# Fewer plain w_out units between the gating stages, more seven-product end groups, and w_sp blocks converted by ScalarE column by column

## The chip, the cores and the metric

The kernel runs on one core of a Trainium2 chip. The metric is device time in microseconds for one execution, lower is better. A core has five engines with a queue each: TensorE (PE; its weight loads are listed as PEld), VectorE (DVE), ScalarE (ACT), GpSimd (POOL) and SyncE (SP, which here only issues DMAs). An engine takes its own queue strictly in the order in which it was written, so an instruction that waits holds up all that stand behind it on that engine.

## The reference

The function is a pre-norm block with two parts. Part A is a linear attention with a memory over four segments of 512 tokens; part B is a gated MLP, and the change lies in part B (and in the scales that it uses).

```python
h  = x + A(layernorm(x))
z  = gelu(layernorm(h) @ w_in)              # 2048 tokens x 3584
z1 = z[..., :1792]
z2 = layernorm(z[..., 1792:])
g  = einsum('ts,bsf->btf', w_sp, z2) + b_sp[None, :, None]   # mixes the 2048 tokens
out = h + (z1 * g) @ w_out                  # w_out: 1792 x 1024
```

All inputs and the output are bfloat16.

## The kernel before, in words

The program is recorded as a list per engine. `_Recorder.record` works out for each instruction which earlier ones on other engines, and which DMAs, it must wait for, from the memory that it reads and writes; `emit` (lines 196 to 241) then writes the waits and the instructions. Every instruction therefore carries line 210 in the profile, and groups are told apart by the names of their tiles. Nothing reorders the work: the order in the source is the order on each engine.

The stages from the middle on are these.

**z2 and z1 stages.** The z2 stage computes the second half of z and its layernorm; the list `aux` (function `at`) hangs other work on its groups, among it the squares of w_sp for a scale (`sp_norm`, `scale_of`, `scale_end`) and the z1 weight blocks' sums (`sz_sum`, GpSimd). The z1 stage (`z1_step`, line 1198) computes z1 transposed into `Z1T` (feature blocks 0 to 13 of 128 rows, 2048 tokens), with `todo1` (function `on`) as its list of extra work.

**Gating stage, pair 0 and pair 1** (`gate`, line 1086). The 2048 output tokens are taken in two pairs of 1024. A pair is a product of a 2x2 block matrix of w_sp (b11, b12, b21, b22: 512 tokens each, as float16 in `BH`) with z2 (float16, `Z2H`), computed with seven block products instead of eight. The sums of w_sp blocks are t1 = b12 - b11, t2 = b22 - t1, t3 = b22 - b12, t4 = b21 - t2 (`SUMS`, line 1060); those of z2 are SS[0] to SS[3], made for each feature group g of 0 to 6 by `s_sum` (called ss1 to ss4). A product is 8 matmuls of 512 columns into one of the eight PSUM banks. The first product P1 (`p1`, with b11) is copied out, scaled, by ScalarE (`copy1` into the tile tmp_s) because several outputs need it alone; after that the b21 product (`p2`) is accumulated into the same bank. GpSimd adds the bias rows `BROW` to the copy (tmp_s1b), VectorE combines banks with these (`stt`: scalar_tensor_tensor into tmp_u) and multiplies by z1 (`out`; `c11` is the pair of these two for the first quadrant). Pair 0 writes bfloat16 back into Z1T, pair 1 float16 into `Z1X`, which is the same memory.

**Units** (lines 1267 and 1331 to 1361) stand between the two gating stages. A unit is 128 tokens by 512 output columns: 14 matmuls of the gated z1 with w_out (`out_unit`), VectorE's add of the residual tile `FIN`, and a store. The residual was loaded by `fin_load` from the output buffer. There are four FIN tiles, so a load waits for the store of four units back. Loads, stores, and the loads of w_out's second half (`WO1`) all go through ScalarE's DMA queue. Behind the units' adds stand the conversions of pair 1's w_sp blocks: DMA transposes on SP (`sp_load`, four for each block, of 128 of its 512 rows each) bring them as bfloat16 into the memory of pair 0's blocks as these come free; `sp_half` scales and casts a whole block on VectorE (4096 elements in a row), `sp_sum` makes the sums. ScalarE computes squares of w_out (`wo_norm`) and of b_sp (`brow_sq`) for scales (`scale_y`, `scale_w`). All of pair 0, 1024 tokens by 1024 columns, is computed by 16 units.

**End groups** (lines 1363 to 1501). Pair 1's product with w_out is again computed by seven block products, in four groups of 2 x 128 tokens, 49 matmuls each. The blocks of w_out are scaled to float16 by ScalarE (`ob_scale`) and their sums made by VectorE (`ob_sum`) inside gating stage 1, by `each1`; the sums of the gated z1 (`y_sum`, tiles SY) belong to each group. ScalarE copies the first product out (`o_p1`), GpSimd adds the residual to it three times (`o_adds`, tiles OT4).

Of the kernel before, what the change touches and what calls it, by code (L numbers as in the profile page):

```python
# [12 lines left out]
T = 2048  # L13
# [20 lines left out]
class _Recorder:  # L34


    def __init__(self, nc):
# [9 lines left out]
        self.out_dmas = []  # L47
        for k in ENGS:
            setattr(self, k, _Eng(self, k))
# [37 lines left out]
    def record(self, eng, name, args, kw, dma=None):  # L87
# [94 lines left out]
        if dma is not None:  # L182
# [4 lines left out]
            key = (aps_out[0] is sb, sb.tensor.name, int(sb.offset))  # L187
# [8 lines left out]
    def emit(self):  # L196
# [9 lines left out]
        def run(eng, e):  # L206
            for op in self.ops[eng]:
                for o in op.waits:
                    e.wait_ge(o.dma if o.dma is not None else sems[o.eng], o.val)
                ins = getattr(e, op.name)(*op.args, **op.kw)  # L210
                if op.dma is not None:
                    ins.then_inc(op.dma, 16)
                elif op.sig:
                    ins.then_inc(sems[eng], 1)
# [44 lines left out]
def bass_sequential_preLN__memory_aug_infini_attn__mixer_gmlp__prompt_kernel(  # L259
# [126 lines left out]
    SQ = b3("sq", [128, 16], F32)  # L386
# [6 lines left out]
    TW, YS, INVY, SCW, INVO = [b3(k, [128, 1], F32) for k in ("tw", "ys", "invy", "scw", "invo")]  # L393
    SQY = tens("sqy", [128, 28], F32, 768)
    BSQ = tens("bsq", [128, 2], F32, 896)
# [5 lines left out]
    WO1 = [tens("w_out1%d" % i, [128, 7, 512], BF16, o * K) for i, o in enumerate((30, 4))]  # L401
    WO0H = [tens("w_out0h%d" % i, [128, 7, 512], F16, o * K) for i, o in enumerate((54, 198))]
    FIN2 = tens("fin2", [128, 4, 2, 2, 512], BF16, 14 * K)
    OT4 = [[tens("ot%d%d" % (i, k), [128, 512], F32, (o + 2 * k) * K) for k in range(4)] for i, o in enumerate((38, 118))]
# [533 lines left out]

    def scale_of(k, n, b):
# [4 lines left out]
        if k:  # L944
            dve.reciprocal(TOP[:], TOT[:])
        else:
            pool.tensor_tensor(TOP[:], TOT[:], MHZ[:], ALU.pow)
# [53 lines left out]
    at(37, pool.tensor_copy, SQB[:, 0:16], SQ[:])  # L1001
# [6 lines left out]
    at(20, pool.tensor_copy, SQB[:, 0:14], SQZ[:])  # L1008
    at(25, scale_of, 1, 14, None)
    at(25, scale_end, 1)  # L1010
    for k in range(8):
# [3 lines left out]
    for k in (1, 2, 3, 4):  # L1015
        at(35 + k, sz_sum, 0, k)
# [4 lines left out]
    for it in todo:  # L1021
# [6 lines left out]
        if it == (0, 12):  # L1028
            sp_norm_load(0)
# [29 lines left out]

    SUMS = {"t1": ("b12", "b11"), "t2": ("b22", "t1"), "t3": ("b22", "b12"), "t4": ("b21", "t2")}  # L1060
# [25 lines left out]
    def gate(pr, seam=lambda: None, mid=lambda: None, each=lambda g, k: None):  # L1086
        inv, zo = (INV[0], Z1T) if pr == 0 else (INVY, Z1X)
# [31 lines left out]
        if not pr:  # L1119
            p1(2)  # L1120
        seam()
        p2(0)
        c11(0)
        for g in range(7):
# [6 lines left out]
            ss(4, g)  # L1131
# [3 lines left out]
            if 1 - pr <= g <= 3:  # L1135
# [14 lines left out]
            out(u3, g, 1, t2)  # L1150
            if not g:
                ss(1, 1)
                ss(2, 1)
            if g < 6:
# [23 lines left out]
    def out_unit(u, wsl, q=sp):  # L1178
        tc, lo, w = u
        b = next_bank()  # L1180
        mm8(PS[:, b, 0:w], lambda i: Z1T[:, i, tc * 128:(tc + 1) * 128], wsl, n=14)
        fin = fins[u]
        dve.tensor_tensor(fin[:, 0:w], fin[:, 0:w], PS[:, b, 0:w], ALU.add)
# [7 lines left out]
    wout = B_w_out.rearrange("(c p) n -> p c n", p=128)  # L1191
# [55 lines left out]
    on(1, 7, scale_of, 0, 16, None)  # L1247
    on(2, 2, scale_end, 0)
    for k, g, r in (("b11", 6, 3), ("b12", 6, 3), ("b22", 8, 3), ("b21", 12, 3)):
# [17 lines left out]
    units = [(tc, 0, 512) for tc in range(6)] + [(tc, 512, 512) for tc in range(8)] + [(tc, 0, 512) for tc in (6, 7)]  # L1267
# [9 lines left out]
    def z1_norm(g, k):  # L1277
        for h in range(k and 2):
            r, o = 2 * g + (k > 2), 1024 + 512 * h
            if k != 2:  # L1280
                act.activation(bank(7), Z1T[:, r, o:o + 512], ACTF.Square, accum_out=SQY[:, 2 * r + h:2 * r + h + 1])

    gate(0, seam, mid, z1_norm)
    pool.tensor_copy(TW[:], TOT[:])
    fin_load(units[0], act)
    fin_load(units[1], act)
    for k in ("b11", "b12", "b22", "b21"):
        for j in range(4):
            sp_load(1, k, j)
    brow_load(1, act)  # L1290
    for i in range(2):
        act.dma_start(WO1[i][:], wout[:, 7 * i:7 * i + 7, 512:D])
# [240 lines left out]
```

## Time and profile before

| | us |
|---|---|
| Median of three runs | 758.01 (757.65 to 758.52) |
| The profiled execution's own time | 757.02 |
| Its span, first to last instruction | 755.3 |
| Gating stage, pair 0, on the weight loads | 489.1 to 574.0 |
| Units | 574.0 to 622.4 |
| Gating stage, pair 1 | 622.4 to 709.3 |
| End groups | 709.3 to 752.4 |

The granted TensorE clock was 1.000 over the span. The profile is of one execution; "busy" for TensorE is modelled, since matmuls overlap, so rates are better read from the starts of successive weight loads. A wait is read as "who waited <- who released it". The stage limits in the table are where the weight loads change from one pair of tiles to the next.

### The profile page before, as it was taken

Reading aid. Unit: us, or ns where it says so; the run is one execution under the profiler, and the core shown is the slowest. Engines: PE = TensorE matmul, PEld = TensorE weight load, DVE = VectorE, ACT = ScalarE, POOL = GpSimd, SP = SyncE. Lnnn points to the kernel's source line nnn. Section 1 sums busy time; section 2 is a strip of 40 time slices with the busy share of each in tenths; the row PEclk is TensorE's granted clock in tenths of the full one; section 3 lists DMA queues with packets and bytes.
Section 4 is the critical chain, followed back from the end, with each engine's and each line's share of the span. In section 5 each row is a group of like instructions: output and inputs, shape, how many; then the busy total and the mean of one; then the engine's idle time right before and its main releaser. Section 6 shows DMA issues by size and latency. Waiting matters only on the chain.

```text
span 755.3 us, 13486 instructions
## 1 busy us (share of the span) xinstructions
PE 748.4 (99%) x5470; PEld 357.9 (47%) x5470; DVE 573.4 (76%) x1013; ACT 421.4 (56%) x519; POOL 294.0 (39%) x450
## 2 busy tenths in 40 slices
PE   8999999999999999999999999999999999999998
PEld 4445455555554445555554444444444444443444
DVE  5585589768974576768896796998895575999876
ACT  6777877787777767226994879723330525300000
POOL 2564456555654333010049988522120001122342
PEclk9999999999999999999999999999999999999999
DMA  9654556454424331678640026320029950001111
GB/s 304 173 160 91 85 78 139 94 79 92 113 58 96 115 72 43 178 195 254 195 141 0 1 56 126 68 86 1 0 41 171 234 196 15 0 1 55 64 49 56
DMA packets 136783, 75.09 MB, mean 99 GB/s; under 512 B 98064, under 2 KB 126480, under 8 KB 136720
## 3 DMA queue, kind: packets, MB, share of 16 engines
q1 hardware_dynamic: 129184, 67.14, 36.9%
q10 hardware_dynamic: 7536, 7.08, 3.2%
q8 instruction: 43, 0.70, 0.4%
q14 instruction: 20, 0.16, 0.1%
HBM read 42.74 MB, written 8.39 MB: 68 GB/s over the span
## 4 chain that ended last, share of the span: by engine, by line
PE 88%; DVE 10%; DMA 1%; issue 1%; POOL 0%; ACT 0%; ACTq 0%; DVEq 0%; POOLq 0%
PE ps L210 88%; DVE z1x L210 3%; DVE tmp_u L210 3%; DVE ss L210 2%; DMA wv<-in_A_wv_dram 1%; DVE tmp_s1b L210 1%; DVE z2h L210 0%; POOL ot L210 0%; DVE sy L210 0%; POOL sy L210 0%; ACT L210 0%; DVE ot L210 0%; DVE fin L210 0%; ACTq L210 0%; DVEq L220 0%
## 5 line engine op out<-in xcount | busy, mean ns | idle before, releaser
L210 ACT ACTIVATE e<-ps 128x2048 bf16<-128x2048 f32 (+1 forms) x96 | 152.7, 1590 | 41.7 <-PE ps L210 41.5
L210 POOL TENSOR_SCALAR_AFFINE_SELECT e<-e 128x512 bf16<-128x512 bf16 x128 | 90.6, 721 | 131.4 <-ACT e L210 131.4
L210 PE MATMUL ps<-win,hnT 128*128 128x448 bf16 x512 | 98.4, 353 | 0.0
L210 POOL TENSOR_TENSOR tmp_s1b<-tmp_s,brow 128x512 f32<-128x512 f32 x28 | 33.6, 1203 | 129.7 <-DVE tmp_u L210 57.4
L210 PEld LDWEIGHTS ps<-win,hnT 128*128 128x128 bf16 x512 | 49.6, 98 | 46.3 <-issue 0.2
L210 PE MATMUL ps<-xnT,wk 128*128 128x512 bf16 x256 | 60.8, 381 | 0.0
L210 PE MATMUL ps<-xnT,wq 128*128 128x512 bf16 x256 | 60.5, 379 | 0.0
L210 PE MATMUL ps<-wv,xnT 128*128 128x512 bf16 x256 | 59.8, 380 | 0.4 <-DVE xnT L210 0.3
L210 DVE TENSOR_TENSOR zt<-ps,zt 128x512 f32<-128x512 f32 x70 | 48.2, 689 | 15.7 <-PE ps L210 12.1
L210 PE MATMUL ps<-wo,oT 128*128 128x512 bf16 x256 | 58.0, 380 | 0.0
L210 ACT ACTIVATE z<-ps 128x448 bf16<-128x448 f32 x60 | 30.6, 548 | 35.0 <-PE ps L210 35.0
L210 PE MATMUL ps<-w_out,z1T 128*128 128x512 bf16 x224 | 48.6, 379 | 0.0
L210 DVE BATCH_NORM_STATS2 zst<-z 128x6 f32<-128x448 bf16 x64 | 38.0, 612 | 10.9 <-ACT z L210 10.9
L210 PEld LDWEIGHTS ps<-v,e 128*128 128x128 bf16 x1280 | 38.8, 96 | 14.0 <-issue 6.5
L210 DVE RECIPROCAL rd<-ps 128x16 f32<-128x16 f32 x32 | 8.0, 250 | 47.1 <-PE ps L210 46.9
L210 ACT ACTIVATE tmp_s<-ps,invy 128x512 f32<-128x512 f32 x7 | 4.8, 687 | 68.0 <-POOL tmp_s1b L210 37.8
L210 PE MATMUL ps<-v,e 128*128 128x33 bf16 x1280 | 42.2, 178 | 0.0
L210 POOL TENSOR_TENSOR sz<-wzh 128x512 f16<-128x512 f16 x28 | 34.5, 1231 | 8.4 <-PE ps L210 8.4
L210 PEld LDWEIGHTS ps<-wo,oT 128*128 128x128 bf16 x256 | 24.0, 98 | 27.6
L210 PEld LDWEIGHTS ps<-xnT,wk 128*128 128x128 bf16 x256 | 22.6, 98 | 29.9 <-issue 5.0
L210 ACT ACTIVATE z1T<-zt,inv 128x512 bf16<-128x512 f32 x42 | 29.0, 715 | 13.1 <-DVE zt L210 13.1
L210 PEld LDWEIGHTS ps<-wv,xnT 128*128 128x128 bf16 x256 | 23.1, 98 | 27.3 <-DVE xnT L210 0.8
(206 smaller groups left out, 1478.0 us busy)
## 6 DMA issues: line engine op xcount, KB each, us to landing
sj<-in_B_w_sp_dram SPq DMA_DIRECT2D x16, 512.0 KB, 3.6
xch<-in_A_x_dram SPq DMA_DIRECT2D x16, 256.0 KB, 3.4
xr<-in_A_x_dram SPq DMA_DIRECT2D x16, 256.0 KB, 3.9
out_dram<-hch SPq DMA_DIRECT2D x16, 256.0 KB, 2.6
win<-in_B_w_in_dram SPq DMA_DIRECT2D x4, 896.0 KB, 5.3
wz<-in_B_w_in_dram SPq DMA_DIRECT2D x6, 512.0 KB, 7.9
wo<-in_A_wo_dram SPq DMA_DIRECT2D x1, 2048.0 KB, 8.4
fin<-out_dram ACTq DMA_DIRECT2D x16, 128.0 KB, 3.0
```

The costliest lines, as they stand in the source:

```text
L210: ins = getattr(e, op.name)(*op.args, **op.kw)
```

## The change

Pair 0 is no longer finished by units alone. Eight units do tokens 0 to 255 and 512 to 767 (token blocks 0, 1, 4, 5 of 128, by two column halves); the other half of pair 0 goes to two more end groups, so six end groups in place of four. Pair 0's gating therefore writes float16 with the final scale, as pair 1's does, and the scale that it needs (YS) is computed in the z1 stage. The squares of w_out move into gating stage 0 (`w_norm`), half of them of a tile `WOT` that is loaded piece by piece for it on ScalarE's queue. In the units, pair 1's w_sp blocks b11, b12 and b22 are cast by ScalarE (b11 by rows, the other two by 128-column pieces as each transpose brings them) and the sums t1, t2, t3 are made by column pieces, t3 and ss after the last unit; t4 is made inside gating stage 1. The transposes come in the order b11, b21, b12, b22. In gating stage 1 the third P1 product is issued early, and c11 and ss4 of group 0 late. w_out's b12 and b22 blocks are loaded with runs of 256 bytes into the token columns that the units have finished with; t4 of w_out is made in the first end group. WO1 lies elsewhere, and its loads stand ahead of those of BROW. Waits on the same DMA semaphore are merged, and some DMAs share one (`group`).

```diff
             for op in self.ops[eng]:
+                need = {}
                 for o in op.waits:
+                    if o.dma is not None:
+                        need[o.dma] = max(need.get(o.dma, 0), o.val)
+                for o in op.waits:
+                    if o.dma is not None and o.val < need[o.dma]:
+                        continue
                     e.wait_ge(o.dma if o.dma is not None else sems[o.eng], o.val)
                 ins = getattr(e, op.name)(*op.args, **op.kw)
                 if op.dma is not None:
...
-    WO1 = [tens("w_out1%d" % i, [128, 7, 512], BF16, o * K) for i, o in enumerate((30, 4))]
+    WO1 = [tens("w_out1%d" % i, [128, 7, 512], BF16, o * K) for i, o in enumerate((38, 30))]
...
-    FIN2 = tens("fin2", [128, 4, 2, 2, 512], BF16, 14 * K)
-    OT4 = [[tens("ot%d%d" % (i, k), [128, 512], F32, (o + 2 * k) * K) for k in range(4)] for i, o in enumerate((38, 118))]
+    FIN2 = tens("fin2", [128, 6, 2, 2, 512], BF16, 14 * K)
+    OT4 = [[tens("ot%d%d" % (i, k), [128, 512], F32, (o + 2 * k) * K) for k in range(4)] for i, o in enumerate((46, 118))]
...
         if k:
-            dve.reciprocal(TOP[:], TOT[:])
-        else:
-            pool.tensor_tensor(TOP[:], TOT[:], MHZ[:], ALU.pow)
+            pool.tensor_single_scalar(TZ[:], TOT[:], float(2 * T * FH * D * D), ALU.mult)
+        pool.tensor_tensor(TOP[:], TOT[:], MHZ[:], ALU.pow)
...
+    def sp_cast(k, j):
+        c = slice(128 * j, 128 * j + 128)
+        act.activation(BH[k][:, :, c], RAW[k][:, :, c], ACTF.Copy, scale=SC[0][:])
+
+    def sp_csum(o, j):
+        a, b = SUMS[o]
+        c = slice(128 * j, 128 * j + 128)
+        dve.tensor_tensor(BH[o][:, :, c], BH[a][:, :, c], BH[b][:, :, c], ALU.subtract)
...
-        inv, zo = (INV[0], Z1T) if pr == 0 else (INVY, Z1X)
+        inv, zo = INVY, Z1X
...
-        if not pr:
-            p1(2)
+        p1(2)
         seam()
         p2(0)
-        c11(0)
+        if not pr:
+            c11(0)
...
-            ss(4, g)
+            if g or not pr:
+                ss(4, g)
...
-            if 1 - pr <= g <= 3:
+            if 1 <= g <= 3:
...
-            out(u3, g, 1, t2)
+            if pr and not g:
+                ss(4, 0)
             if not g:
                 ss(1, 1)
                 ss(2, 1)
+            out(u3, g, 1, t2)
+            if pr and not g:
+                c11(0)
             if g < 6:
...
-        mm8(PS[:, b, 0:w], lambda i: Z1T[:, i, tc * 128:(tc + 1) * 128], wsl, n=14)
+        mm8(PS[:, b, 0:w], lambda i: Z1X[:, i, tc * 128:(tc + 1) * 128], wsl, n=14)
         fin = fins[u]
-        dve.tensor_tensor(fin[:, 0:w], fin[:, 0:w], PS[:, b, 0:w], ALU.add)
+        dve.scalar_tensor_tensor(fin[:, 0:w], PS[:, b, 0:w], IY[:], fin[:, 0:w], ALU.mult, ALU.add)
         q.dma_start(out2d[tc * 128:(tc + 1) * 128, lo:lo + w], fin[:, 0:w])
...
+    on(9, 3, pool.tensor_tensor, TOT[:], TOT[:], TZ[:], ALU.mult)
+    on(9, 3, pool.tensor_tensor, TOP[:], TOT[:], MHZ[:], ALU.pow)
+
+    def y_scale():
+        dve.tensor_single_scalar(TOP[:].bitcast(I32), TOP[:].bitcast(I32), 0x7F800000, ALU.bitwise_and)
+        dve.tensor_single_scalar(YS[:], TOP[:], 8192.0, ALU.mult)
+        dve.tensor_tensor(INVY[:], INV[0][:], YS[:], ALU.mult)
+        dve.reciprocal(IY[:], YS[:])
+
+    def brow_scale():
+        for k in range(2):
+            act.activation(BROW[k][:], BROW[k][:], ACTF.Copy, scale=YS[:])
+
+    on(11, 2, y_scale)
+    on(11, 3, brow_scale)
     for k, g, r in (("b11", 6, 3), ("b12", 6, 3), ("b22", 8, 3), ("b21", 12, 3)):
...
-    units = [(tc, 0, 512) for tc in range(6)] + [(tc, 512, 512) for tc in range(8)] + [(tc, 0, 512) for tc in (6, 7)]
+    units = [(tc, lo, 512) for lo in (0, 512) for tc in (0, 4, 1, 5)]
...
+    def w_sq(c, v):
+        act.activation(bank(7), v, ACTF.Square, accum_out=SQY[:, c:c + 1])
+
+    def w_norm(g, k):
+        h = 4 * g + k
+        if h % 2:
+            w_sq(14 + h // 2, WOT[:])
+        else:
+            act.dma_start(WOT[:], wout[:, h // 2, 512:D])
+            for c in ([h // 2 - 2] if h >= 4 else []) + ([h // 2] if h >= 24 else []):
+                w_sq(c, WO0[c // 7][:, c % 7, :])
+
+    def w_scale(n):
+        if n == 0:
+            pool.tensor_copy(SQB[:], SQY[:])
+        if n == 1:
+            b = 3
+            pe.matmul(PS[:, b, 0:28], ONES[:], SQB[:], start=True, stop=True)
+            dve.tensor_reduce(out=TOT[:], in_=PS[:, b, 0:28], axis=mybir.AxisListType.X, op=ALU.add)
+            dve.tensor_single_scalar(TOT[:], TOT[:], 1e-30, ALU.max)
+            pool.tensor_tensor(TOP[:], TOT[:], MHZ[:], ALU.pow)
+        if n == 3:
+            dve.tensor_single_scalar(TOP[:].bitcast(I32), TOP[:].bitcast(I32), 0x7F800000, ALU.bitwise_and)
+            dve.tensor_single_scalar(SCW[:], TOP[:], 8192.0, ALU.mult)
+            dve.tensor_tensor(INVO[:], YS[:], SCW[:], ALU.mult)
+            dve.reciprocal(INVO[:], INVO[:])
...
+    gate(0, seam, mid, w_norm)
+    for u in units[:2]:
+        fin_load(u, act)
+    for i in range(2):
+        act.dma_start(WO1[i][:], wout[:, 7 * i:7 * i + 7, 512:D])
+    brow_load(1, act)
+    for k in ("b11", "b21", "b12", "b22"):
         for j in range(4):
             sp_load(1, k, j)
-    brow_load(1, act)
...
+    for r in range(4):
+        sp_part("b11", r)
+
+    rot["n"] = 0
     for n, u in enumerate(units):
-        if n + 2 < 16:
+        if n + 2 < 8:
             fin_load(units[n + 2], act)
         out_unit(u, (lambda i: WO0[i // 7][:, i % 7, :]) if u[1] == 0 else
                  (lambda i: WO1[i // 7][:, i % 7, :]), act)
...
+        w_scale(n)
...
-        if n == 1:
-            sp_half("b11")
-        if n == 4:
-            sp_half("b12")
-            sp_sum("t1")
-        if n == 6:
-            sp_half("b22")
-            sp_sum("t3")
-        if n == 8:
-            sp_sum("t2")
-        if n == 10:
+        if n == 2:
             sp_half("b21")
-            sp_sum("t4")
-        if n == 12:
-            scale_w()
-        if n == 13:
-            for k in range(1, 4):
-                s_sum(k, 0)
...
+        if n in (4, 5):
+            for j in (2 * n - 8, 2 * n - 7):
+                sp_cast("b12", j)
+                sp_csum("t1", j)
+        if n == 5:
+            brow_scale()
+        if n in (6, 7):
+            for j in (2 * n - 12, 2 * n - 11):
+                sp_cast("b22", j)
+                sp_csum("t2", j)
+    for k in range(1, 4):
+        s_sum(k, 0)
+    for j in range(4):
+        sp_csum("t3", j)
+
+    W4 = {"b12": (Z1T, 0), "b22": (Z1T, 1), "t1": (Z2, 0), "t2": (Z2, 1), "t3": (Z1T, 0), "t4": (Z2, 2)}
...
+    def ob_load(k):
+        i = 7 if k == "b22" else 0
+        R.group = (k,)
+        w = wout[:, i:i + 7, 512:D].rearrange("p c (a b t) -> p c a b t", a=2, b=2)
+        o = ob(k, 0, 7, False).rearrange("p (c a) b t -> p c a b t", a=2)
+        for a in range(2):
+            for b in range(2):
+                sp.dma_start(o[:, :, a, b], w[:, :, a, b])
+        R.group = None
...
+    GR = [(0, 2), (0, 3)] + [(1, j) for j in range(4)]
...
+    for n, o in enumerate(("t1", "t2", "t3")):
+        for m in range(4):
+            jobs.setdefault(((2, 2, 2, 3, 3, 3, 3, 4, 4, 4, 5, 6)[4 * n + m], 0), []).append((ob_sum, o, 2 * m))
...
+    ob_load("b12")
+    ob_load("b22")
+    gate(1, mid=mid, each=each1)
...
-    fin_in(2)
-    fin_in(3)
+    for g in range(2, 6):
+        fin_in(g)
     o_p1(0)
-    for x in range(1, 4):
-        y_sum(x, 0, 6, 7)
     o_adds(0)
-    o_prod(3, o_s(2, 0), "t2", True, cs=range(6))
+    o_p1(1)
+    o_prod(3, o_s(2, 0), "t2", True)
     o_p2(0)
     o_c11(0)
...
-    for g in range(4):
+    for g in range(6):
         bb, bc = 3 + g % 2, 5 + g % 2
-        last = ((bc, 0, 512),) if g < 3 else ((bc, 0, 384), (7, 384, 512))
+        last = ((bc, 0, 512),) if g < 5 else ((bc, 0, 256), (7, 256, 512))
...
+        if g == 0:
+            for m in range(4):
+                ob_sum("t4", 2 * m)
+        if g < 3:
+            o_p1(g + 2)
         o_prod(bb, o_s(3, g), "t3", False)
-        if g < 3:
-            o_p1(g + 1)
-        elif g == 3:
-            o_p2(3)
+        if g < 4:
+            o_adds(g + 1)
+            o_p2(g + 1)
```

## The prediction

> **What bounds the kernel now.** I read the page first (busy shares, then the chain that ended last), then the weight loads of TensorE in the last gating stage, then the timeline between the two gating stages.
>
> ```profile
> PE 748.4 (99%) x5470; PEld 357.9 (47%) x5470; DVE 573.4 (76%) x1013; ACT 421.4 (56%) x519; POOL 294.0 (39%) x450
> PE 88%; DVE 10%; DMA 1%; issue 1%; POOL 0%; ACT 0%; ACTq 0%; DVEq 0%; POOLq 0%
> ```
>
> TensorE carries 88% of the chain, VectorE 10%. That 10% is one stretch, 634.9 to 716.1 us: the second gating stage. The waits of its weight loads (window 622 to 709; us in total, times, longest):
>
> ```profile
> PEld ps L210 <- DVE tmp_u L210: 4.3, 6, 1.1
> ```
>
> So TensorE idles there for VectorE's tmp_u, the sums out of the product banks. And the timeline between the stages (start, us, engine, what; in brackets the idle time before it):
>
> ```profile
> 573.97 24.05 PEld L210 LDWEIGHTS ps<-w_out,z1T 128*128 128x128 bf16 x112
> 574.89 10.38 SPq L210 DMA_TRANSPOSE b22r<-in_B_w_sp_dram  x4
> 577.61 1.11 ACTq L210 DMA_DIRECT2D w_out<-in_B_w_out_dram  x2
> 578.75 4.14 ACTq L210 DMA_DIRECT2D fin<-out_dram  x1
> 585.31 9.83 SPq L210 DMA_TRANSPOSE b21r<-in_B_w_sp_dram  x4
> 590.90 0.69 DVE L210 TENSOR_TENSOR fin<-fin,ps 128x512 bf16<-128x512 bf16 x1 [7.40 <-DMA fin<-out_dram]
> 591.38 0.33 ACTq L210 DMA_DIRECT2D fin<-out_dram  x1
> 594.56 0.69 DVE L210 TENSOR_TENSOR fin<-fin,ps 128x512 bf16<-128x512 bf16 x1 [2.07 <-DMA fin<-out_dram]
> ...
> 622.36 3.34 PEld L210 LDWEIGHTS ps<-b11h,z2h 128*128 128x128 f16 x16
> 624.50 0.69 ACT L210 ACTIVATE tmp_s<-ps,invy 128x512 f32<-128x512 f32 x1 [14.33 <-PE ps L210]
> 625.82 1.61 PEld L210 LDWEIGHTS ps<-b21h,z2h 128*128 128x128 f16 x8
> 627.54 1.61 PEld L210 LDWEIGHTS ps<-t2h,ss 128*128 128x128 f16 x8
> ```
>
> To be seen: 16 units run from 573.97 to 622.36, 48.4 us, without a gap. Eight matmuls of 512 columns take 627.54 - 625.82 = 1.72 us (1.727 over longer stretches): 0.2158 us each. The third fin load was issued at 578.75 behind the two w_out loads and VectorE got it only at 590.90; the next fin load needs the first store landed and arrives at 594.56. All this is hidden now, since the w_sp conversions have 48 us and run on VectorE. The copy at 624.50 follows the first product at once, and the b21 product (which adds onto the bank that was copied) need not wait.
>
> **What the Trainium skill says.** "DMA: Bandwidth & Descriptors", section "Queues, rings and completion order": SP and ACT own one ring each per DMA engine, consumed in ring order, and an engine takes turns between rings by packets. The trace agrees: the fin load waited out 1.8 MB ahead of it on ACT's ring (12.1 us from issue to use; the page's median to landing is 3.0). "TensorE: Matmul & The Clock Gate", section "Step-by-step: what each phase is for": about 216 ns from one 512-column matmul to the next; here 215.8. "ScalarE: Activation LUTs", section "What ACT_TABLE_LOAD costs": neighbouring ACTIVATEs overlap by about 93 ns; here casts of 128x1024 last 1.14 us and follow each other after 1.05. "DMA: Bandwidth & Descriptors", section "Specifications": full rate needs runs of 512 B; the new b12/b22 loads of w_out have runs of 256 B. No run here shows them; the nearest row is wz with 256 B runs, 256 KB in 4.8 us. Taking some 2 us of that as fixed, 2.8 us for 1024 runs give an estimated 20 us for the 7168 runs, issued from about 597 and wanted from 618: covered, with little to spare.
>
> **The change, part by part.**
>
> *Products.* Units fall from 16 x 14 = 224 to 112 matmuls; end groups rise from 4 x 49 = 196 to 294. Net -14 x 0.2158 = **-3.0 us**. This is certain.
>
> *Norms moved.* Gate 0 keeps 28 ScalarE squares (0.79 us with the read) and gains 14 loads of 128 KB on ACT's queue. ScalarE idles 8.5 us per group there, so it is free except at the end: after the last copy (561.26) three load-then-square rounds of about 4.5 us follow, so the last square ends near 575.2 instead of 567.1. Then come the fin loads (574.4 before, now 575.2). The w_out loads stand ahead of brow now: about 576.5 against 577.6. The scale chain moved into the z1 stage is four VectorE operations (0.65 us) and two ScalarE ones (1.3 us), where VectorE has gaps of only 0.17 us: 0 to 0.5, I take **+0.2**. Reading z1 as f16 and scaling in the final add (0.75 against 0.69 us) cost nothing on TensorE.
>
> *Units.* The SP queue issues b21 at 571 (its last reader), then b12, b22: 12 transposes, 25.9 us from 569.2 to 595.1 before, so until about 597, landed by 602. Not the bound. ScalarE is. Its queue now holds, in order: fin loads, w_out, brow, four b11 casts (4.3 us), then per unit a fin load, the output store (which waits for VectorE's add) and two casts. VectorE in turn queues two column sums behind each add, and they wait for those casts. From unit 4 on it is a loop: store issue 0.45, casts 1.05 + 1.14, sum 0.05 + 0.65, next add 0.75: **4.1 us a unit**, TensorE 3.02.
>
> When does it start? Fin load 2 follows w_out and brow in ACT's ring: I take 590.0 (590.9 before; w_out is issued about 1 us sooner). Fin load 4 waits for store 0, is issued at 590.5, lands 3.1 later, unit 4's add ends at 594.3. Stores 5, 6 and 7 are issued by 598.85, 602.95, 607.05; the last casts end at 609.25; only then comes the gating copy, 0.69: 609.9. The b21 product accumulates into that copied bank, so it waits. TensorE, unhindered, would get there at 573.97 + 24.2 + 3 x 1.727 = 603.35. **+6.55 us.** (w_out's second half, wanted at 587.6 and landing near 589.5, stalls unit 4 by 1.8; that is inside these 6.55.) Sums and the two ss blocks end at 611.25, the b21 product at 611.6: hidden behind it.
>
> *Gate 1.* VectorE works 10.3 us a group (656.04 to 667.89 less three sums of 0.51), TensorE 12.1, or 10.4 in groups 0 and 4 to 6, where the P1 product came earlier. After the wait VectorE still owes ss3, four t3 sums, four t4 sums (0.61 each, 5.5 us) and the postponed c11 and ss4. Walked through by these durations, the group-1 t3 product waits 1.9 us net for the add before it (VectorE 17.4 us after the start, TensorE 15.5). Group 2 and 3 sums fit; the three at group 4 exceed it by 1.8. Together 3.7 against 2.4 before (the six waits sum to 4.3, of which the weight-load pipeline regains 0.2 to 0.4 each: 622.36 to 709.34 is 86.98, less 392 x 0.2158): **+1.3**.
>
> *End.* 0.8 us is lost at 713.8 and 716.1 now, because the first adds run uncovered. A second P1 product ahead covers them, and the first group is ready earlier: **-0.7**. The four t4 sums (2.5 us) end 1.3 us before their product. The last bank's half is 256 columns instead of 128: **+0.1**.
>
> Sum: -3.0 + 0.2 + 6.55 + 1.3 - 0.7 + 0.1 = +4.4. On the profiled execution's 757.02 (span 755.3) that is 761.4; the median 758.01 lies 1.0 above it: **762.4**.
>
> **Rivals.** 0.2% (1.5 us) is about what a measurement of this kernel can tell from no change.
>
> *A, ScalarE's loop delays the b21 product,* as above, 760 to 765: chance 0.50. For it: the 7.40 us wait at 590.90. Against it: the transposes' order differs, so the ring may drain sooner.
>
> *B, the loop keeps pace: faster.* One mechanism: fin load 2 lands early, so casts follow the loads and the copy ends before 603.35. The copy follows fin load 2 by 19.9 us, so the point is a landing at 583.4. Then -3.0 + 0.2 + 1.3 - 0.7 + 0.1 = -2.1: 755.9. For it: 1 MB of transposes used to be issued from 574.9, while now b21 has been issued by 576.7. Against it: the w_out loads alone bring 1.8 MB, and the 576 to 590 stretch moved 64 to 364 GB/s. Chance 0.20.
>
> *C, half of the wait:* landing near 586.5, about 758: chance 0.14.
>
> *D, VectorE or a load is later still:* the brow issue blocks ACT as the fin load did at 578.75 (4.14 us), so the b11 casts start 4 us later and all behind them; or the 256 B loads hold up the scaling in group 1 and the copy behind it. 765 to 769: chance 0.16.
>
> **How the numbers follow.** Faster 0.20 (B), within 0.2% 0.12 (most of C), slower 0.68 (A, D, the rest of C). The range from 755.2 to 766.5 takes in B, C, A and part of D. A alone: 760 to 765.
>
> **What would show it.** Right: the b21 product of gate 1 idle before it, released by ScalarE's tmp_s, some 5 to 8 us; fin adds in the units waiting for DMA fin; stores of units 5 to 7 some 4 us apart; about 3.7 us of VectorE waits in gate 1. Wrong: fin load 2 landing before 584; the b21 product following at once; the t2 product waiting for the t2 sums because b22 lands late; end groups longer than 10.6 us each.

## The result, and the profile after

The changed kernel takes 767.45 us (median of four runs, 765.96 to 768.62) against 758.07 of the kernel before on the same chip (757.65 to 758.52): ratio 1.0123, 95% interval 1.0104 to 1.0141. It is 9.4 us slower. The forecast was 762.4 us, 755.2 to 766.5: the right side, by about half of what came, and the median lies 1 us outside the range.

The profiled execution took 768.62 us, its span is 766.9. Section 1 of the page (busy time) and section 4 (chain that ended last) now read:

```profile
PE 750.1 (98%) x5455; PEld 358.6 (47%) x5455; DVE 585.1 (76%) x1032; ACT 421.7 (55%) x517; POOL 301.1 (39%) x450
PE 85%; DVE 9%; DMA 2%; issue 1%; ACT 1%; ACTq 1%
```

DMA, ScalarE (ACT) and its queue (ACTq) hold more of the chain than before: 2%, 1% and 1% against 1%, 0% and 0%. The busy time of TensorE did not fall although it has 15 matmuls fewer: some ran at half rate, as shown below (2.5 us), and the part ahead of gating stage 0, which is left out below, has 1.9 us more of it (488.7 against 486.7). The waits of the weight loads from the units to the end (window 574 to 766; total, times, longest) say who is in the chain:

```profile
PEld ps L217 <- ACT tmp_s L217: 6.5, 1, 6.5
PEld ps L217 <- DVE tmp_u L217: 5.3, 5, 2.1
PEld ps L217 <- issue: 3.6, 13, 0.3
PEld ps L217 <- DMA w_out<-in_B_w_out_dram: 2.4, 2, 2.1
PEld ps L217 <- DVE ot L217: 1.1, 1, 1.1
```

One wait of 6.5 us is for ScalarE's tmp_s, the copy of the first gating product. It is the wait that the prediction named. The 13 "issue" gaps of 0.28 us are new, and are the half rate. The timeline of ScalarE between the stages (start, us, engine, what; in brackets the idle time before it) shows how the copy comes so late:

```profile
585.34 0.45 ACTq L217 DMA_DIRECT2D out_dram<-fin  x1
...
593.82 0.34 ACTq L217 DMA_DIRECT2D fin<-out_dram  x1
...
597.97 0.34 ACTq L217 DMA_DIRECT2D fin<-out_dram  x1
598.35 0.70 ACTq L217 DMA_DIRECT2D out_dram<-fin  x1
599.10 1.15 ACT L217 ACTIVATE b12h<-b12r,sc 128x1024 f16<-128x1024 bf16 x1 [11.76 <-issue]
...
602.70 0.35 ACTq L217 DMA_DIRECT2D out_dram<-fin  x1
...
606.70 0.37 ACTq L217 DMA_DIRECT2D out_dram<-fin  x1
...
610.73 0.34 ACTq L217 DMA_DIRECT2D out_dram<-fin  x1
...
613.20 0.67 ACT L217 ACTIVATE tmp_s<-ps,invy 128x512 f32<-128x512 f32 x1
```

For 11.8 us before its first b12 cast at 599.10 ScalarE computes nothing: its queue stands at fin loads that need a landed store (593.82, 597.97) and at stores that need an add. The adds of units 2 and 4 on VectorE waited for these loads:

```profile
593.34 0.75 DVE L217 SCALAR_TENSOR_TENSOR fin<-ps,iy,fin 128x512 bf16<-128x512 f32 x1 [9.39 <-DMA fin<-out_dram]
597.16 0.75 DVE L217 SCALAR_TENSOR_TENSOR fin<-ps,iy,fin 128x512 bf16<-128x512 f32 x1 [0.58 <-DMA fin<-out_dram]
```

Then the stores come 4.0 us apart, and the copy is at the end of that row. What TensorE does with it, in the weight loads from the end of the units on:

```profile
602.38 5.06 PEld L217 LDWEIGHTS ps<-b11h,z2h 128*128 128x128 f16 x24
613.92 0.13 PEld L217 LDWEIGHTS ps<-b21h,z2h 128*128 128x128 f16 x2 [6.48 <-ACT tmp_s L217]
614.32 0.15 PEld L217 LDWEIGHTS ps<-b21h,z2h 128*128 128x128 f16 x1 [0.28 <-issue]
...
619.86 1.61 PEld L217 LDWEIGHTS ps<-t1h,ss 128*128 128x128 f16 x8
...
635.70 1.41 PEld L217 LDWEIGHTS ps<-t3h,ss 128*128 128x128 f16 x8 [2.15 <-DVE tmp_u L217]
```

After the wait, the 16 matmuls of the b21 and t2 products take 619.86 - 613.92 = 5.94 us, or 2.49 more than 16 x 0.2158 = 3.45. Twelve steps in a row, 614.32 to 619.43, are 0.43 us each, twice the usual, and the granted clock from 613.92 to 619.43 is 0.50. The Trainium skill describes this in "TensorE: Matmul & The Clock Gate", "Part 1: The HAM clock gate": after an idle window of some 3.4 us the clock falls to half, and it comes back after about 3.4 us of work, which varies from run to run. The trace agrees in kind: 6.5 us idle, then half rate until 619.43, 5.5 us.

Where the time went. The profiled execution's gate 0 starts at 491.55 against 489.13, all of it from the first 20 us, where TensorE's granted clock was 0.91 against 1.00 and 1.37 us against 0.68 were spent on a load of wv. Code there is the same, and in the experiments below, which share that code, gate 0 starts between 489.0 and 490.4; so I leave it out and count from the start of the units (573.97 before, 576.39 after) to the end of the span: 181.33 us before, 190.51 after, **+9.18**, close to the 9.4 of the medians.

| from the units' start on, us | predicted | measured |
|---|---|---|
| 14 matmuls fewer | -3.0 | -3.02 |
| b21 product later than unhindered (29.38 after the start) | +6.55 | 37.53 - 29.38 = +8.15 |
| 16 matmuls at half rate | not seen | +2.49 |
| gate 1 waits for VectorE | +1.3 | 3.84 net against 2.4: +1.44 |
| start of the end stage | -0.7 | 0.74 lost against 0.54: +0.2 |
| tail | +0.1 | -0.1 |
| sum | +4.25 | +9.16 |

### The profile page after: what moved, and what is told of

Its sections match the earlier page's. It is cut to its first block, busy times and chain, and to the rows that moved or that the text cites. A ratio compares the mean times of both kernels' runs of the same rounds, so it can differ in the third digit from the quotient of the medians.

```text
span 766.9 us, 13491 instructions
## 1 busy us (share of the span) xinstructions
PE 750.1 (98%) x5455; PEld 358.6 (47%) x5455; DVE 585.1 (76%) x1032; ACT 421.7 (55%) x517; POOL 301.1 (39%) x450
## 4 chain that ended last, share of the span: by engine, by line
PE 85%; DVE 9%; DMA 2%; issue 1%; ACT 1%; ACTq 1%
PE ps L217 85%; DVE tmp_u L217 3%; DVE z1x L217 2%; DMA out_dram<-fin 2%; DVE ss L217 1%; ACTq L217 1%; DVE z2h L217 1%; DMA wv<-in_A_wv_dram 1%; DVE tmp_s1b L217 1%; ACT b12h L217 1%; ACT b22h L217 0%; DVE fin L217 0%; DVE ot L217 0%; DVE sy L217 0%; ACT b11h L217 0%
## 5 line engine op out<-in xcount | busy, mean ns | idle before, releaser
L217 ACT ACTIVATE tmp_s<-ps,invy 128x512 f32<-128x512 f32 x14 | 9.6, 685 | 97.2 <-POOL tmp_s1b L217 70.8
L217 POOL TENSOR_TENSOR ot<-ot,fin 128x512 f32<-128x512 f32 x18 | 22.9, 1301 | 42.7 <-ACT ot L217 22.2
L217 ACT ACTIVATE ot<-ps,invo 128x512 f32<-128x512 f32 x6 | 4.1, 687 | 61.8 <-PE ps L217 61.8
L217 DVE TENSOR_TENSOR z1x<-tmp_u,z1T 128x512 f16<-128x512 f32 x42 | 36.5, 868 | 1.4
```

## The experiments

Two theories were to be told apart. *Mine*: the order of ScalarE's queue makes the loss, because stores, loads and casts in one queue wait for each other. *The rivals*: the half rate of TensorE is the larger part; or VectorE, which has the same row of sums, would have been as late without ScalarE. Medians of before on the chip used were 758.3 to 758.6 us throughout.

**TensorE kept busy.** 24 extra matmuls into an unused bank fill most of the wait; their results are not used.

```diff
         p1(2)
+        if pr:
+            for x in range(24):
+                pe.matmul(bank(7), a_blk(0, 0, 0)[:, x % 8, :], BH["b11"][:, x % 8, :], start=True, stop=True)
         seam()
```

> The changed kernel with 24 extra matmuls of 512 columns into a bank that nobody reads, placed between the third P1 product and the b21 product of gating stage 1, so that TensorE works through most of the 6.4 us in which it now waits for ScalarE's copy. Nothing else moves: the copy is as late as before. Theory (the 16 weight loads after the wait run at half rate because TensorE had stood still): they run at 0.216 us each again, 2.5 us are saved, 764.9 against 767.4. Rival (the slow stretch comes from something else near it, such as the GpSimd and VectorE work at that place): no gain, 767.4.

Measured: 766.66 us (766.3 to 766.99), ratio 1.011 [1.0093, 1.0127]. The weight loads that waited, from the end of the units on:

```profile
612.84 1.41 PEld L217 LDWEIGHTS ps<-b21h,z2h 128*128 128x128 f16 x8 [1.19 <-ACT tmp_s L217]
615.16 1.41 PEld L217 LDWEIGHTS ps<-t2h,ss 128*128 128x128 f16 x8 [0.91 <-DVE ss L217]
619.78 1.41 PEld L217 LDWEIGHTS ps<-t3h,ss 128*128 128x128 f16 x8 [1.49 <-DVE tmp_u L217]
634.02 1.41 PEld L217 LDWEIGHTS ps<-t3h,ss 128*128 128x128 f16 x8 [2.47 <-DVE tmp_u L217]
```

The half rate is gone, but little of its 2.5 us came back: 0.8 us by the medians, where the runs of the changed kernel themselves lie 2.7 us apart, and 0.1 us from the units' start to the end of the two profiled executions (190.43 against 190.51, with the copy itself 0.5 us later in the first). The t2 and t3 products, which followed at once after the slow stretch, now wait 0.91 and 1.49 us for VectorE, and group 1 waits 0.3 longer. So the slow stretch mostly lay over a lateness of VectorE that was there anyway.

**VectorE converts b12 and b22 whole**, as in the kernel before. This undoes the part of the change that gave the column casts to ScalarE.

```diff
-        if n in (4, 5):
-            for j in (2 * n - 8, 2 * n - 7):
-                sp_cast("b12", j)
-                sp_csum("t1", j)
+        if n == 4:
+            sp_half("b12")
+            sp_sum("t1")
...
-        if n in (6, 7):
-            for j in (2 * n - 12, 2 * n - 11):
-                sp_cast("b22", j)
-                sp_csum("t2", j)
+        if n == 7:
+            sp_half("b22")
+            sp_sum("t2")
```

> The changed kernel with one part undone: b12 and b22 are scaled and cast by VectorE as whole blocks (1.28 us each) and t1, t2 made as whole blocks (2.3 us each), b12 after unit 4, b22 after unit 7; ScalarE has no casts in the units but those of b11. Theory (the copy is late because ScalarE's stores and casts alternate with VectorE's adds): the copy follows the store of unit 7 at about 604.4, the b21 product does not wait, TensorE keeps its clock: about 8.5 us less, 759. Rival (b22's transposes land late and bound the t2 sums whoever casts them): the wait moves to the t2 product and 764 or more remain.

Measured: 761.29 us (760.58 to 763.04), 1.0044 [1.0029, 1.0059]: 6.2 of the 9.4 us are back. The weight loads at the t2 and t1 products:

```profile
609.20 0.13 PEld L217 LDWEIGHTS ps<-t2h,ss 128*128 128x128 f16 x2 [2.98 <-DVE ss L217]
...
612.57 1.39 PEld L217 LDWEIGHTS ps<-t1h,ss 128*128 128x128 f16 x7 [0.25 <-issue]
```

The b21 product follows at once. The t2 product does wait 2.98 us for VectorE's sums, and half rate follows that too, until 612.57. ScalarE's queue, in which stores and casts alternate, is the larger cause; without it VectorE is still late by 3 us.

**Eight FIN tiles**, so that no load waits for a store; all eight loads stand ahead of the units, four of them ahead of w_out.

```diff
-        k = len(fins) % 4
+        k = len(fins) % 8
-    for u in units[:2]:
+    for u in units[:4]:
         fin_load(u, act)
     for i in range(2):
         act.dma_start(WO1[i][:], wout[:, 7 * i:7 * i + 7, 512:D])
     brow_load(1, act)
+    for u in units[4:]:
+        fin_load(u, act)
-        if n + 2 < 8:
-            fin_load(units[n + 2], act)
```

> The changed kernel with eight residual tiles in place of four: units 0 to 3 load theirs ahead of w_out, units 4 to 7 behind the bias rows, none waits for a store. Stores and casts stay on ScalarE. Theory (the loop of store, casts, sums and add starts late because the fifth residual waits for the first store, which waits behind w_out's 1.8 MB): the first cast starts at the end of unit 4, some 3.6 us earlier, and the wait of the b21 product falls from 6.4 to about 2.8 us; short enough to keep the clock, so 761; 763.8 if the clock drops all the same. Rival (the loop's own 4 us per unit is all of it): 766 or more.

Measured: 765.42 us (762.91 to 765.9), 1.0089 [1.0072, 1.0106]. The b21 wait falls from 6.48 to 2.52 us, and no half rate follows. But the units wait 2.53 and 2.13 us for w_out, against 0.25 and 2.11, and the t2 and t3 products of group 0 wait 0.91 and 1.50 us for VectorE, as in the run with extra matmuls. That the four fin loads ahead of w_out make it later is not shown: the next run has the same order, and waits 0.88 and 2.10 us. Only 2 us are gained; the casts still stand behind stores.

**The same, and the stores go out on SP's queue.**

```diff
         out_unit(u, (lambda i: WO0[i // 7][:, i % 7, :]) if u[1] == 0 else
-                 (lambda i: WO1[i // 7][:, i % 7, :]), act)
+                 (lambda i: WO1[i // 7][:, i % 7, :]), sp)
```

> As the kernel with eight residual tiles, but the units' stores are issued by SP, behind its transposes, so that ScalarE no longer waits for VectorE's adds. Theory: casts run back to back as the transposes land, the copy is done before TensorE wants the b21 product, no wait and no half rate: -3.0 for the products, +1.8 for w_out's arrival, +0.5 to 1.5 in gating stage 1, 757.5 to 759. Rival (the transposes of b22 land too late): a wait of 3 us or more at the t2 product, 761 or more.

Measured: 760.64 us (757.22 to 764.4, twenty runs), 1.0026 [1.0014, 1.0038]. Of the slowdown of 1.23%, 0.26% is left. The profiled execution, 757.99 us, is the third fastest of the twenty; what the slower ones lose beyond it is not on record. ScalarE's timeline:

```profile
597.45 4.25 ACT L217 ACTIVATE b22h<-b22r,sc 128x1024 f16<-128x1024 bf16 x4
602.73 0.69 ACT L217 ACTIVATE tmp_s<-ps,invy 128x512 f32<-128x512 f32 x1 [1.02 <-PE ps L217]
```

The four b22 casts stand back to back, 1.06 us each, and the copy waits for TensorE: the wait has turned round. The eight stores on SP stand behind the transposes and go out only from 597.96 on, which holds up nothing now that each unit has a tile of its own. ScalarE's casts as such are not slow; the waits of its DMA issues in the same queue were. The waits for w_out (0.88 and 2.10 us) and in group 1 (2.15 us) remain.

**The copy alone made early.** In the changed kernel, the first two P1 products and the copy go between units 3 and 4, and GpSimd's two bias adds to unit 5; gating stage 1 leaves them out in turn.

```diff
         w_scale(n)
+        if n == 3:
+            prod(0, a_blk(0, 0, 0), "b11", True)
+            act.activation(TMP["s1"][:], bank(0), ACTF.Copy, scale=INVY[:])
+            prod(1, a_blk(0, 0, 1), "b11", True)
...
         if n == 5:
             brow_scale()
+            pool.tensor_tensor(TMP["s1b2"][:], TMP["s1"][:], BROW[1][:], ALU.add)
+            pool.tensor_tensor(TMP["s1b1"][:], TMP["s1"][:], BROW[0][:], ALU.add)
```

> The changed kernel with the first two P1 products of gating stage 1 issued between units 3 and 4, the copy of the first right behind on ScalarE, and GpSimd's two adds of the bias rows after these have been scaled, in unit 5. Stores and casts stay as they are. If the late copy alone made the loss: the b21 product does not wait, w_out's arrival (1.8 us) is covered by the two products, and the time falls to about 758.5. If, as the run with extra matmuls suggests, the t2 sums and the ss blocks on VectorE end as late as the copy: the wait of the b21 product goes to the t2 product (about 612 to 613.5 instead of 616.9, since the ss blocks then run without GpSimd beside them at 0.68 us instead of 1.5 to 1.6), 763 to 765.

Measured: 765.65 us (764.82 to 766.25), 1.009 [1.0075, 1.0105]. On the weight loads, and then on VectorE's timeline:

```profile
614.20 0.13 PEld L217 LDWEIGHTS ps<-t2h,ss 128*128 128x128 f16 x2 [8.44 <-DVE ss L217]
```

```profile
612.74 0.69 DVE L217 TENSOR_TENSOR ss<-z2h 128x1024 f16<-128x1024 f16 x1
613.46 0.69 DVE L217 TENSOR_TENSOR ss<-ss,z2h 128x1024 f16<-128x1024 f16 x1
614.06 0.68 DVE L217 TENSOR_TENSOR ss<-z2h 128x1024 f16<-128x1024 f16 x1
```

The b21 product no longer waits, and the t2 product waits 8.44 us in its place, for sums that stand behind the same casts: the last t2 sum began at 612.13, after the last b22 cast. The copy was only the first in the row to be waited for. This settles that the whole loop of casts, stores, adds and sums was late, and not one instruction of it. And it shows a second thing: the three ss sums take 0.69 us here, where the changed kernel has 1.53 and 1.63 for two of them. There, GpSimd's two bias adds run at that time, here they ran earlier. The next section comes back to it.

**What is left.** The other seven runs start from the version with eight FIN tiles and stores on SP, and move the remaining waits.

*P1 as a cover for w_out:* two P1 products between units 3 and 4 (without the copy).

```diff
         w_scale(n)
+        if n == 3:
+            prod(0, a_blk(0, 0, 0), "b11", True)
+            prod(1, a_blk(0, 0, 1), "b11", True)
```

> Eight residual tiles and stores on SP as in the fourth run, and the first two P1 products between units 3 and 4 (the copy stays behind the units). It tells what w_out's late arrival costs by itself. Theory: the 2.3 us that TensorE waits in unit 4 are covered by 3.5 us of products: 1 to 2.3 us less than the fourth run, the rest perhaps taken back because VectorE's ss blocks still follow the last unit and now have 3.5 us less before the t2 product. Rival (all of it comes back at the t2 product): no gain.

Measured: 762.15 us (759.63 to 763.08), 1.0043 [1.0023, 1.0062]: no gain. P1 waits for ScalarE's b11 casts, one after another (2.31, 0.93, 0.91 and 0.91 us), since ScalarE issues brow and fin loads until 587.8 before it casts; a short stretch at half rate follows.

*ss sums early:* the second half of w_out goes to other memory, so that the SS tile is free and its three sums can be made behind unit 1.

```diff
-    WO1 = [tens("w_out1%d" % i, [128, 7, 512], BF16, o * K) for i, o in enumerate((38, 30))]
+    WO1 = [tens("w_out1%d" % i, [128, 7, 512], BF16, o * K) for i, o in enumerate((38, 4))]
...
+        if n == 1:
+            for k in range(1, 4):
+                s_sum(k, 0)
...
-    for k in range(1, 4):
-        s_sum(k, 0)
```

> Eight residual tiles and stores on SP as in the fourth run, and w_out's second half in the memory of the gating temporaries (as before the change) instead of that of ss, so that ss1 to ss3 of gating stage 1 are made after unit 1 and not after the last. It tells what the ss blocks at the seam cost (0.69, 1.61 and 1.64 us in the fourth run, the latter two beside GpSimd's bias adds). Theory: VectorE enters gating stage 1 some 4 us ahead, the wait of the t3 product of group 1 (2.15 us) goes, 1.9 us less than the fourth run. Rival (the backlog comes from the t3 and t4 sums and c11, and is only moved): under 0.7 us less.

Measured: 760.22 us (757.44 to 761.39), 1.0017 [1.0005, 1.0029]. The group-1 wait is 2.14 us as before, and the time is 0.4 us less than without this edit: the rival's reading.

*This, the P1 cover, and w_out's sums spread otherwise over the groups* (1, 1, 1, 2, 2, 2, 3, 3, 3, 4, 5, 5 in place of 2, 2, 2, 3, 3, 3, 3, 4, 4, 4, 5, 6).

> The seventh run's edits with the P1 products between units 3 and 4 as in the sixth, and the twelve sums of w_out blocks in gating stage 1 spread as 3, 3, 3, 1, 2 over groups 1 to 5 instead of 3, 4, 3, 1, 1 over groups 2 to 6, since groups 4 to 6 have only six products (10.4 us) over VectorE's 10.3. Theory: no wait for w_out, none at group 1, about half of the 2.4 us lost at groups 3 to 5: some 4 us less than the fourth run's profile, 754 to 755.5, faster than both kernels. Rival (the DMA transposes then bound the t2 sums): 757 or more, with a wait of the t2 product.

Measured: 761.06 us (758.45 to 762.96), 1.0032 [1.0024, 1.004]. P1 waits for the b11 casts again (3.08 us and three times 0.93), and group 1 has a further wait of 1.26 us. Not a gain.

*t4 sums early:* from behind the first add of gate 1 to directly behind the t3 sums.

```diff
     for j in range(4):
         sp_csum("t3", j)
+    for r in range(4):
+        sp_sum("t4", r)
...
-    gate(1, mid=mid, each=each1)
+    gate(1, each=each1)
```

> The run with the early ss sums, with the four t4 sums moved from behind the first add of gating stage 1 to directly behind the t3 sums. Theory (the 2.1 us wait of the group-1 t3 product is VectorE's backlog from the t4 sums): that wait falls to under 0.5 us, the t4 sums cost at most 0.5 us at the group-0 t3 product, and the time falls by some 1.5 us, to about 758.7. Rival (the same 2.5 us of VectorE work is only late at another place): group 1's wait goes, but group 0's t3 product or the group-1 b21 product waits as long; time 760 to 760.5.

Measured: 760.61 us (759.0 to 763.8), 1.0029 [1.0014, 1.0044]. The group-1 wait stays at 2.15 us, so it is not made by the t4 sums either. In its profiled execution w_out came later than in that of the run with early ss sums (waits of 2.92 and 1.53 us against one of 1.74, and half rate after the first), so the times of these two executions can't be set against each other.

*b11 casts first, P1 cover, t4 early:* ScalarE casts b11 ahead of its brow loads and of the last four fin loads.

```diff
-    brow_load(1, act)
-    for u in units[4:]:
-        fin_load(u, act)
     for k in ("b11", "b21", "b12", "b22"):
         for j in range(4):
             sp_load(1, k, j)
     for r in range(4):
         sp_part("b11", r)
+    brow_load(1, act)
+    for u in units[4:]:
+        fin_load(u, act)
```

> The run with early t4 sums, with two P1 products of gating stage 1 placed between the fourth and fifth unit, and ScalarE's four b11 casts placed ahead of its brow and last four fin loads. Theory (the P1 cover failed before only because the b11 casts stood behind blocked loads): P1 follows the units at once, the second w_out wait (2.1 us) is hidden, and the time falls by 1.5 to 2 us, to about 757. Rival (the transposes of b11 are late, or the last four fin loads now are): P1 waits for b11h, or the fin adds of units 4 to 7 and the casts behind them come later, and nothing is gained; time 759 to 762.

Measured: 759.12 us (758.36 to 761.15), 1.0009 [1.0, 1.0018]. P1 follows unit 3 at once, the first half of w_out is covered, the second still costs 2.26 us, and the t3 product of group 0 waits 2.34 us for the first add, which now stands behind the t4 sums.

*The same with w_out's sums* at 1, 1, 2, 2, 2, 2, 3, 3, 3, 3, 4, 5:

> As the run before, with the twelve sums of w_out blocks spread over groups 1 to 5 as 2, 4, 4, 1, 1 in place of groups 2 to 6 as 3, 4, 3, 1, 1. Theory (three sums in group 4, which has no spare VectorE time, cost some 1.5 us in waits of groups 4 and 5): another 1 us, about 756. Rival (VectorE's lateness is set by its whole load after the start and not by where these sums stand): the waits move to groups 2 and 3, same time within 0.5 us.

Measured: 759.85 us (758.07 to 761.26), 1.0017 [1.001, 1.0024]. The waits of groups 4 and 5 go from 3.0 (0.84, 0.99, 1.14) to 2.0 us (1.14, 0.87), and three of 0.66 to 0.69 appear in groups 1 to 3. No gain: the waits move with the sums, as the rival said.

*b11 casts first, P1 cover, t4 sums back behind the first add:*

> The run with the P1 cover and the b11 casts first, with the four t4 sums back behind the first add of gating stage 1 (early ss sums kept). Theory (at the seam VectorE sets the pace in the run with early t4: the 2.5 us of t4 sums ahead of the first add are what the group-0 t3 product waited 2.3 us for): that wait falls to 0.5 us or less, the group-1 wait stays near 2.1 to 2.4, and the time falls by 1.5 to 2 us, to about 757.3, level with or just under the kernel before. Rival (VectorE's whole work from the last unit to group 1 is what counts, wherever t4 stands): the 2.3 us reappears in group 1's t3 wait, 4 us or more, and the time stays at 759.

Measured: 757.93 us (756.09 to 759.08, fourteen runs) against 758.35, ratio 0.9991 [0.9982, 1.0]. This is the best version that I found, and it is level with the kernel before rather than better. Its waits from the units to the end:

```profile
PEld ps L217 <- DVE tmp_u L217: 5.3, 5, 2.1
PEld ps L217 <- DMA w_out<-in_B_w_out_dram: 1.4, 1, 1.4
PEld ps L217 <- DVE ot L217: 1.1, 1, 1.1
PEld ps L217 <- DVE t2h L217: 0.7, 1, 0.7
```

These make 8.5 us. The same view of the kernel before has 4.3 for tmp_u, 0.9 for ot and 0.2 for GpSimd's sy: 5.4. The difference of 3.1 is the 3.0 us that the seven-product groups save. From the units' start to the end the two profiled executions take 181.4 and 181.33 us.

What makes the 2.15 us of group 1 can be counted in the traces. VectorE's row from the second add of group 0 to the add that the group-1 t3 product waits for, in the kernel before and in the changed one:

```profile
634.87 0.75 DVE L210 SCALAR_TENSOR_TENSOR tmp_u<-ps,invy,tmp_s1b 128x512 f32<-128x512 f32 x1 [3.83 <-PE ps L210]
...
643.92 0.75 DVE L210 SCALAR_TENSOR_TENSOR tmp_u<-ps,invy,tmp_s1b 128x512 f32<-128x512 f32 x1
```

```profile
623.73 0.75 DVE L217 SCALAR_TENSOR_TENSOR tmp_u<-ps,invy,tmp_s1b 128x512 f32<-128x512 f32 x1 [0.30 <-PE ps L217]
...
625.18 1.08 DVE L217 TENSOR_TENSOR ss<-z2h,ss 128x1024 f16<-128x1024 f16 x1
...
628.23 0.75 DVE L217 SCALAR_TENSOR_TENSOR tmp_u<-ps,invy,brow 128x512 f32<-128x512 f32 x1
629.01 0.69 DVE L217 TENSOR_TENSOR z1x<-tmp_u,z1T 128x512 f16<-128x512 f32 x1
...
634.90 0.75 DVE L217 SCALAR_TENSOR_TENSOR tmp_u<-ps,invy,tmp_s1b 128x512 f32<-128x512 f32 x1
```

At 623.73 VectorE had been waiting for TensorE, so whatever stands ahead of it is worked off. From there to 634.90 it works without a gap on fifteen operations, 11.17 us; in the kernel before there are twelve, 9.05 us. The three more are ss4 of group 0 and the pair of c11 (shown above), which the change puts off to this place. TensorE reaches the t3 product 9.94 us after the first of these adds in both kernels, so the 2.12 us more are the wait. This also says why the ss and t4 sums did not move it: they stand ahead of the stretch. In all ten profiles that have 2.14 or 2.15 us, VectorE comes to that add on time, and in eight of them it waits there for TensorE. It is a count, not an experiment: to put c11 or ss4 of group 0 elsewhere was not tried.

## Why the prediction was right and wrong

The wait, its cause and most of its length were forecast. What failed is the step after it: the prediction took the matmuls behind the wait at full rate and VectorE's sums as "hidden behind it", and so put nothing in the sum for either. TensorE ran at half rate instead, which cost 2.49 us, and behind it VectorE was late as well, so that taking the half rate away alone gave 0.8 us or less. To this come two terms of the wrong size: the wait, 1.6 us too small, and the end stage, a gain of 0.7 us that did not come.

**Products: right.** -3.02 us.

**The wait at the b21 product: mechanism right, 1.6 us too small.** It idles for ScalarE's tmp_s, 6.48 us in one piece, the fin adds wait for DMA fin, and the stores of units 5 to 7 are 4.00 to 4.03 us apart against 4.1 predicted. The step that was mis-sized is "When does it start?". Counted from the units' start, fin load 4 was issued at 17.4 instead of 16.5: it needed the first store, issued at 585.34 behind 1.8 MB of w_out, and was let go at 593.82. The unit-4 add, which needs this load, ended at 21.5 instead of 20.3, and the first b12 cast began at 22.7 instead of 20.8. Of the last 0.7, 0.4 is fin load 6 (597.97 to 598.31), which stands ahead of store 4 on ScalarE and which my sum left out; most of the rest is the issue of store 4, 0.70 us instead of 0.45. The loop made up 0.3 again, at 4.0 instead of 4.1 us a unit. The 1.8 us of w_out inside this term came as forecast.

**Not in the sum: TensorE restarts at half rate.** +2.49 us on the profile. I predicted an idle of 6.5 us and priced the work behind it at full rate. The run with TensorE kept busy shows that 0.8 us of it or less is to be had by removing it alone, because the next step was wrong too:

**"Sums and the two ss blocks end at 611.25 ... hidden behind it": wrong.** It took 0.68 us for an ss sum. These two took 1.53 and 1.63 us. The two views, VectorE and GpSimd of the changed kernel:

```profile
614.66 1.53 DVE L217 TENSOR_TENSOR ss<-ss,z2h 128x1024 f16<-128x1024 f16 x1
616.11 1.63 DVE L217 TENSOR_TENSOR ss<-z2h 128x1024 f16<-128x1024 f16 x1
```

```profile
613.95 3.25 POOL L217 TENSOR_TENSOR tmp_s1b<-tmp_s,brow 128x512 f32<-128x512 f32 x2 [29.37 <-ACT tmp_s L217]
```

GpSimd's two bias adds run from 613.95 to 617.20, started by the same copy that TensorE waited for. Each took 1.6 us; alone one takes 1.16 (624.56). The Trainium skill, "SBUF — State Buffer", section "SBUF: two separate sides", says that a VectorE operation with two SBUF inputs and a GpSimd one that reads SBUF take a shared pair of ports in turn, each for the whole instruction. The times agree: the bias adds end at 615.64 and 617.20, and the two ss sums each 0.55 us later, at 616.19 and 617.74. The run with the early copy is the counter-check, 0.69 us for the same sums with GpSimd idle. The profile of the kernel before showed it in gate 0 (1.52 us for an ss sum at 494.50, two bias adds of 2.96 us from 492.51), and I took the duration from a row without this neighbour.

**Gate 1: the size right, the reason only in part.** 3.7 us of VectorE waits were predicted and 3.84 net came; the group-1 wait was walked out at 1.9 us net and came at 2.15, or 1.8 net of what the weight loads catch up behind it. But the walk summed ss3, the t3 and t4 sums and the postponed pieces, and by the count at the end of the experiments only the postponed c11 and ss4 make the wait. That both come to about 2 us is luck.

**End stage: wrong.** -0.7 was predicted. The second P1 product did cover the first adds, but a new wait of 1.07 us for ot at the t4 product took its place. "End 1.3 us before their product" is the step that failed: the four t4 sums took 3.18 us (708.83 to 712.0) instead of 2.5, and the sum of the gated z1 just ahead of them 1.43 (707.47) against 0.62 for others of its shape, both beside five GpSimd adds of 6.43 us from 703.49. So the add behind them, which the product needs, ended only at 712.67. The port as the reason here is argued from these durations; no run took the GpSimd adds away.

**Rivals.** B (faster) fell: fin load 2 was used at 593.3, not 583.4. C fell with it. A had the mechanism, and its upper end of 765 was 2.5 us short. D gave the time, 765 to 769, but not by what it named: the brow issue lasted 2.7 us, the b11 casts were in time (583.07 to 587.3), and the 256-byte loads held nothing up. "Slower" was right at 0.68.

Not settled: how much of the 9.4 us belongs to each cause alone. ScalarE's casts give 6.2 us when they are undone; eight FIN tiles with stores on SP give 6.8; the half rate gives 0.8 or less. These overlap, since behind each wait stands another that is nearly as long.

## What to carry to other kernels

When work is moved to an engine that also issues DMAs, walk through its queue with every issue and what that issue waits for; a store behind an add and a load behind a store turn free time into a lock-step loop with another engine. Here eight residual tiles and the stores on another queue together gave back 6.8 of 9.4 us. After a predicted idle of several us, price TensorE's next matmuls at half rate (12 steps of 0.43 us here, after 6.48 us), and look for the next engine in the row, since a wait that is removed alone often passes to it. Take durations from rows with the same neighbours: a two-input VectorE sum beside GpSimd's bias adds took 1.53 and 1.63 us instead of 0.68.

## What was not expected of the hardware

- From the units on, half rate came after single idles of 8.44, 6.48, 2.98 and 2.92 us, and not after single ones of 2.53 us and less. It also came at the end of two rows of waits, of 2.31 and 3.08 us and then three of about 0.92 (the two runs in which P1 waits for the b11 casts). The two idles of 2.9 us lie below the window of some 3.4 us that the Trainium skill's section on the clock gate gives; the measurement decides. After the first three idles it lasted 3.7, 5.5 and 3.4 us; the fourth stretch was cut short by the next wait.
- Four DMA transposes of 256 KB took 13.11 us to issue (b12, from 578.68 on) beside 1.8 MB of w_out loads, and 15.64 in the run with stores on SP; the four of b21 just ahead of them took 5.29.
- A store of 128 KB, issued at 585.34 behind those loads, let the load that waited for it go only at 593.82; the median from issue to landing on the page is 1.7 us for the 23 stores of this size on SP and 3.8 us for the eight on ScalarE's queue.
- Moving eight stores from ScalarE's queue to SP's, with nothing else changed, was worth 4.8 us on the medians (765.42 to 760.64).
